# Router logits of three token tiles in one pass, gate weights held in three column strips of the array

## The chip, the cores and the metric

The kernel runs on one core of one Trainium2 chip. The metric is the device time of one launch in microseconds (us). TensorE is called PE here, its weight loads PEld; VectorE is DVE, ScalarE is ACT, GpSimd is POOL, SyncE is SP.

## The reference

A block-sparse attention feeds a mixture of experts. Cut to what matters:

```python
# attention: B, H, S, D = 4, 8, 768, 64; blocks of 32 rows; window, first, last and 3 sampled blocks are kept
scores = np.where(mask, scale * np.matmul(q, k.transpose(0, 1, 3, 2)), -1000000000.0)
attn = np.exp(scores - np.max(scores, axis=-1, keepdims=True))
attn = attn / (np.sum(attn, axis=-1, keepdims=True) + 1e-09)
x = np.matmul(attn, v)                      # reordered to N, D = 3072, 512

# experts: E, F = 8, 1024
logits = x @ w_gate
noise_scale = np.log1p(np.exp(x @ w_noise))
noisy_logits = logits + noise_scale * noise
top2 = np.argpartition(-noisy_logits, 2, axis=1)[:, :2]
...                                         # softmax weights of the two chosen experts
h = np.maximum(x[mask] @ w1[e], 0.0)
out[mask] += top2_w[mask, k, None] * (h @ w2[e])
```

The change touches only how `x @ w_gate` and `x @ w_noise` are laid on the engines.

## The kernel before, in words

**Two stages.** First comes attention, in 64 steps. A step ("macro") is four heads of one tile of 128 query rows. 24 token tiles come out of it, in four sets of T = 6 tiles. When a set is complete a routing job (`Router.run`, a generator) is advanced a few instructions at a time between the pieces of later steps (`background`); a job has one matmul group on line 635 to 639 and two on line 713. The second stage is the experts: nine blocks of rows with two matmul layers each.

**A step in program order.** `Attention.steps` writes, for step n: scores of n (PE, line 215), their row maximum (DVE, lines 250 and 269); then the transposes of step n-1's probabilities (PE, line 303, copied out by ACT, line 305); then the exponentials of n (ACT, line 291); then attention times values of n-2 (PE, line 318), then the normalisation of n-2 (DVE, lines 360 to 379). `step(n, spot)` is called with spot 0 to 3 between these pieces. Spot 1 lies behind the transposes and ahead of line 318, spot 2 behind line 318.

**A token tile behind attention.** A tile is finished every second step. Its rows are transposed by PE two steps later in four 128x128 pieces (`Router.turn`, line 548) and copied from PSUM into the tile `r_xT` (DVE, line 550). One step later `Router.logits` forms the 16 logits of each row: four accumulating matmuls with the tile as the stationary operand (128x128, fp32) and the gate weights `r_wgn` as 16 moving columns (line 560), then a small copy into `r_lc` (DVE, line 562). Both are called at spot 1. The six tiles of `r_lc` start the set's job.

**What is shared.** The PSUM tile `pe` has one buffer: transposed rows, logits and the job's matmuls use it in turn, and each waits until DVE has read the one before. While a job holds it (`router.held`), new tiles first advance the job.

**What POOL and the queues do.** For each half of a unit POOL starts an indirect load of values (`va`, line 189), behind a tiny copy `tick` (line 421) that waits for the row maximum of that step, and then copies twelve sampled key blocks next to the others (`kv`, line 205). The scores two steps later read these. Values by window (`vb`) are loaded from ACT's queue, queries from SP's.

**Experts.** From the third block on `fast1` uses seven products where there would be eight; its intermediate sums sit in tiles `um` (line 1044) and `r_xT` (line 1047), and the sums of weights in `s3` (line 862).

Of the kernel before, what the change touches and what calls it, by code (L numbers as in the profile page):

```python
# [9 lines left out]
F32 = mybir.dt.float32  # L10
# [8 lines left out]
P = 128  # L19
# [8 lines left out]
E = 8  # L28
# [5 lines left out]
OVC = OVT * P  # L34
NC = 7
NSLOT = NV * OVC
BIGIDX = 1 << 20

class Attention:
# [429 lines left out]
class Router:  # L469
# [12 lines left out]

    def consts(self, w_gate, w_noise, noise):
        nc, pool, T, B, KB = self.nc, self.pool, self.T, self.B, self.D // P
        wgn = self.wgn = pool.tile([P, KB, 2 * E], F32, name="r_wgn")
        nc.sync.dma_start(wgn[:, :, 0:E], w_gate.rearrange("(k p) e -> p k e", p=P))
        nc.sync.dma_start(wgn[:, :, E:], w_noise.rearrange("(k p) e -> p k e", p=P))
        self.noise = pool.tile([P, B, T, E], F32, name="r_noise")
        nc.sync.dma_start(self.noise.rearrange("p b t e -> p (b t e)"), noise.rearrange("p i e -> p (i e)"))

    def tables(self):
# [20 lines left out]
        self.spacer = pool.tile([1, 1], F32, name="r_spacer")  # L512
        self.tokf = pool.tile([P, B * T], F32, name="r_tokf")
        nc.vector.tensor_scalar(self.tokf, self.tok, float(-BIGIDX), None, op0=ALU.add)
        self.tab = pool.tile([P, NV * NC, 2], F32, name="r_tab")
        nc.vector.memset(self.tab, 0.0)
        self.sl = pool.tile([P, B * T, 2], I32, name="r_sl")
# [25 lines left out]
    def turn(self, i, xs, pt):  # L543

        nc = self.nc
        xv = xs.rearrange("p h d -> p (h d)")
        for kb in range(self.D // P):
            nc.tensor.transpose(pt[:, kb * P:(kb + 1) * P], xv[:, kb * P:(kb + 1) * P], self.ident)
        self.xT[i] = self.pool.tile([P, self.D // P, P], F32, name="r_xT", bufs=2)
        nc.vector.tensor_copy(self.xT[i].rearrange("p k r -> p (k r)"), pt)  # L550

    def logits(self, i, pl):

        nc, T, KB = self.nc, self.T, self.D // P
        b, t = divmod(i, T)
        if t == 0:
            self.lc[b] = self.pool.tile([P, T, 2 * E], F32, name="r_lc", bufs=2)
        xT = self.xT.pop(i)
        for kb in range(KB):
            nc.tensor.matmul(pl[:, 0:2 * E], xT[:, kb], self.wgn[:, kb], start=kb == 0, stop=kb == KB - 1,  # L560
                             skip_group_check=True)
        nc.vector.tensor_copy(self.lc[b][:, t], pl[:, 0:2 * E])

    def run(self, b, ps):

# [159 lines left out]
class Experts:  # L725
# [130 lines left out]
    def sums(self, e, s, part):  # L856
        tt = lambda o, x, y, f: self.nc.vector.tensor_tensor(o, x, y, op=f)
        a11, a12, a21, a22 = self.sums_raw(e, s)
        top, low = (self.st["wraw", e, j][0] for j in (s, s + 2))
        if part == 0:  # L860
            self.sums_split(e, s, 0, top)
            s3 = self.st["s3", e, s] = self.tsp.tile([P, 2, 256], F32, name="s3", bufs=2)
            tt(s3, a11, a21, ALU.subtract)
            tt(a21, a21, a22, ALU.add)
        elif part == 1:
            self.sums_split(e, s, 4, low)
        elif part == 2:
# [147 lines left out]
    def fast1(self, u, hook):  # L1015
        nc, H = self.nc, C // 2
# [23 lines left out]
        for p in range(self.FB // 2):  # L1040
            mul = lambda *a: self.product(u, p, *a)
            A, B, Cb = (self.ps_m.tile([P, 512], F32, name=n) for n in ("ma", "mb", "mc"))
            mul(A, 0, plain(0, 0), True)
            m = new("um", 2)
            nc.scalar.activation(m, A[:, 0:H], AF.Copy)
            mul(B, 2, mixed(1, 1), True)
            s2 = self.router.pool.tile([P, 4, P], F32, name="r_xT", bufs=2).rearrange("p k r -> p (k r)")[:, 0:H]
            add(s2, B[:, 0:H], m)
            self.flush()
            if self.rest:  # L1050
# [214 lines left out]
def kernel(ctx, tc, q, k, v, v_windows, sampled_blocks, w_gate, w_noise, noise, w1, w2, out):  # L1265
    nc = tc.nc
# [15 lines left out]
    jobs, fresh, flat = [], [], []  # L1282
    started = [0]
    now = [0]

# [7 lines left out]
    def turn_rows(n):  # L1293
        while flat and flat[0][0] <= n:
# [3 lines left out]
            router.turn(i, xs, psum[0]())  # L1298
            fresh.append((n + 1, i))

    def new_logits(n):
        while fresh and fresh[0][0] <= n:
            while router.held:
                background()
            i = fresh.pop(0)[1]
            router.logits(i, psum[0]())
            if i % T == T - 1:
                jobs.append(router.run(i // T, lambda: psum[0]()))
                started[0] += 1

    psum = [att.psum]

# [290 lines left out]
```

## Time and profile before

| | us |
|---|---|
| three timed runs, median (lowest to highest) | 866.12 (864.75 to 867.81) |
| the profiled execution, its own time | 856.92 |
| its span | 855.1 |
| PE busy | 791.1 |
| DVE busy | 549.3 |
| ACT busy | 372.6 |
| POOL busy | 360.2 |
| mean granted clock of PE, share of full speed | 0.969 |

The profiled execution took 9.2 us less than the median of the timed runs, and 1.8 us more than its own span. Attention lies between 0 and about 316 us of the span, the experts behind it. A busy share is an average over both stages.

### The profile page before, as it was taken

How to read it: one execution, taken by the hardware profiler on the slowest of the kernel's cores; microseconds unless marked ns; L12 is line 12 of the kernel's file. 1: busy time of each engine (PE TensorE's matmuls, PEld its weight loads, DVE VectorE, ACT ScalarE, POOL GpSimd, SP SyncE). 2: the span in 40 equal slices, each digit the busy share in tenths (PEclk: the TensorE clock that was granted, in tenths of full speed). 3: DMA queues.
4: the chain of work that ended last, by engine and by line, in shares of the span. 5: the costliest groups of instructions: out<-in, count | busy, mean ns of one | idle time of the engine just before them, and what ended most of it. 6: DMA issues, size and time to landing. Idle time of an engine off the chain costs nothing.

```text
span 855.1 us, 21866 instructions
## 1 busy us (share of the span) xinstructions
PE 791.1 (93%) x8889; PEld 483.4 (57%) x8889; DVE 549.3 (64%) x1122; ACT 372.6 (44%) x678; POOL 360.2 (42%) x555
## 2 busy tenths in 40 slices
PE   4899888889898878989999999999999999999996
PEld 2577676666676766548544544544544544544542
DVE  3555475756767845722558688678787786868741
ACT  2575464555565534301435445445435445435400
POOL 2534552542224520051317526537537546546431
PEclk9999898998998989999999999999999999999998
DMA  8856986695259898557845696695696695796221
GB/s 336 296 187 220 267 244 187 240 365 174 75 148 256 237 170 303 207 141 160 188 147 127 135 255 140 121 246 130 149 238 141 148 249 119 131 241 140 76 80 53
DMA packets 125021, 159.71 MB, mean 187 GB/s; under 512 B 66581, under 2 KB 83221, under 8 KB 124912
## 3 DMA queue, kind: packets, MB, share of 16 engines
q1 hardware_dynamic: 96400, 75.76, 32.6%
q0 software_dynamic: 20016, 57.47, 27.1%
q10 hardware_dynamic: 8496, 25.01, 9.3%
q8 instruction: 72, 1.18, 0.6%
q14 instruction: 37, 0.30, 0.1%
HBM read 117.30 MB, written 27.10 MB: 169 GB/s over the span
## 4 chain that ended last, share of the span: by engine, by line
PE 54%; DMA 1%; issue 1%; POOL 0%; DVE 0%; POOLq 0%
PE py L1083 26%; PE mb L1002 9%; PE ma L1002 6%; PE mc L1002 6%; PE ph L987 5%; PE py L1093 2%; DMA xtb<-xg 1%; PE py L1102 0%; DMA xg<-x_rows,gi 0%; POOL out_dram L1159 0%; DMA out_dram<-y,mt 0%; DVE y L1145 0%; PE pr L1114 0%; POOLq L1179 0%; POOLq L926 0%
## 5 line engine op out<-in xcount | busy, mean ns | idle before, releaser
L1133 POOL DMA_INDIRECT pv<-out_dram,gi x42 | 101.9, 2425 | 95.6 <-ACT pv L1127 49.3
L1002 PEld LDWEIGHTS <-wop 128*128 128x128 f16 x1008 | 98.6, 98 | 76.3
L1083 PEld LDWEIGHTS <-hh 128*128 128x128 f16 x768 | 74.5, 98 | 89.7 <-issue 2.5
L215 PE MATMUL s<-kv,q 64*32 64x192 f32 (+3 forms) x1920 | 95.9, 357 | 22.9 <-DMA kv<-in_k_dram 8.5
L305 ACT ACTIVATE t<-t 128x512 f32<-128x512 f32 (+1 forms) x120 | 63.0, 566 | 85.5 <-PE t L303 82.5
L205 POOL COPY kv<-kv 128x128 f32 x264 | 67.7, 305 | 52.9 <-issue 25.1
L1159 POOL DMA_INDIRECT out_dram<-pv,mt x42 | 51.8, 1233 | 89.2 <-DMA out_dram<-pv,mt 35.3
L1002 PE MATMUL mb<-tx,wop 128*128 128x408 f16 x432 | 83.3, 336 | 0.0
L215 PEld LDWEIGHTS s<-kv,q 64*32 64x32 f32 (+2 forms) x1920 | 52.6, 130 | 45.9 <-issue 16.6
L291 ACT ACTIVATE p<-s,nb 128x256 f32<-128x256 f32 x176 | 69.5, 477 | 19.3 <-DVE nb L269 13.8
L250 DVE TENSOR_REDUCE nm<-s 128x4 f32<-128x1024 f32 (+1 forms) x48 | 54.4, 1133 | 32.3 <-PE s L215 32.2
L1083 PE MATMUL py<-w2h,hh 128*128 128x512 f16 x192 | 72.8, 379 | 0.0
L1083 PE MATMUL py<-w1ha,hh 128*128 128x512 f16 x192 | 72.8, 379 | 0.0
L1083 PE MATMUL py<-w2l,hh 128*128 128x512 f16 x192 | 72.8, 379 | 0.0
L1083 PE MATMUL py<-w1la,hh 128*128 128x512 f16 x192 | 72.8, 379 | 0.0
L303 PE MATMUL t<-ident,p 128*128 128x128 f32 x448 | 69.1, 297 | 3.5 <-ACT t L305 3.5
L1083 PE MATMUL py<-w2h,hl 128*128 128x512 f16 x192 | 68.9, 379 | 0.0
L1083 PE MATMUL py<-w1ha,hl 128*128 128x512 f16 x192 | 68.8, 379 | 0.0
L303 PEld LDWEIGHTS t<-ident,p 128*128 128x128 f32 x448 | 51.2, 148 | 28.0 <-issue 15.7
L1007 ACT ACTIVATE hh<-us 128x408 f16<-128x408 f32 x48 | 26.1, 543 | 91.8 <-DVE us L1023 91.8
L926 POOL DMA_INDIRECT xg<-x_rows,gi x56 | 57.9, 1033 | 15.9 <-issue 15.0
L1083 PEld LDWEIGHTS <-hl 128*128 128x128 f16 x384 | 37.6, 98 | 45.3
(213 smaller groups left out, 1465.1 us busy)
## 6 DMA issues: line engine op xcount, KB each, us to landing
wraw<-in_moe_w_dram SPq DMA_DIRECT2D x64, 512.0 KB, 5.3
vb<-in_v_windows_dram ACTq DMA_DIRECT2D x28, 390.0 KB, 6.3
vb<-in_v_windows_dram ACTq DMA_DIRECT2D x14, 520.0 KB, 4.9
kv<-in_v_dram SPq DMA_DIRECT2D x4, 1560.0 KB, 17.8
q<-in_q_dram SPq DMA_DIRECT2D x12, 512.0 KB, 8.0
kv<-in_k_dram SPq DMA_DIRECT2D x8, 768.0 KB, 11.1
out_dram<-zero ACTq DMA_DIRECT2D x8, 768.0 KB, 5.1
x_rows<-x SPq DMA_DIRECT2D x20, 256.0 KB, 3.4
```

The costliest lines, as they stand in the source:

```text
L205: nc.gpsimd.tensor_copy(KG[:, j, :, 32 * s:32 * s + 32], KT[:, :, bass.ds(offs[3 * j + s], 32)])
L215: mm = lambda out, l, r, pos: nc.tensor.matmul(out, l, r, start=True, stop=True, tile_position=pos)
L250: red = lambda out, x: nc.vector.tensor_reduce(out, x, axis=AX.X, op=ALU.max, negate=True)
L291: self.nc.scalar.activation(p[:, 256 * u:256 * u + 256], S[:, a, 256 * r:256 * r + 256], AF.Exp, bias=nb[:, u:u + 1], scale=0.125)
L303: self.nc.tensor.transpose(T[i][:, c:c + P], p[:, i * w + c:i * w + c + P], self.ident)
L305: self.nc.scalar.activation(t[:, i * w:(i + 1) * w], T[i][:, 0:w], AF.Copy)
L926: g = nc.gpsimd.indirect_dma_start(out=self.xg[0:m, c], out_offset=None, in_=self.x_dram[0:nr], in_offset=bass.IndirectOffsetOnAxis(ap=r[" ...
L987: nc.tensor.matmul(ph[:, b, 0:m], w[wt][:, kb, fs], r["xt"][:, kb, a, o:o + m], start=i == 0, stop=i == last)
L1002: self.nc.tensor.matmul(bank[:, 0:H], w[:, h, o, k, cs], x(k, a), start=start and i == 0, stop=i == len(seq) - 1, skip_group_check=True)
L1083: nc.tensor.matmul(py, h[:, f, o], w[x][:, f, :], start=i == 0, stop=i == last)
L1133: g = nc.gpsimd.indirect_dma_start(out=y[0:m], out_offset=None, in_=self.out, in_offset=bass.IndirectOffsetOnAxis(ap=r["gi"][0:m, c:c + 1] ...
L1159: x = self.nc.gpsimd.indirect_dma_start(out=self.out, out_offset=bass.IndirectOffsetOnAxis(ap=self.st["u", u]["mt"][0:m, c:c + 1], axis=0) ...
```

## The change

`LG` = 3 tiles are put together in the first and second set, and of the third and fourth set the first three tiles (`grouped`): six groups, 18 tiles. For the first two tiles of a group nothing is issued at the place of the logits. At the third, `logits_of_three` holds the gate weights stationary, padded to 32 columns, in three column strips of the array, and streams each transposed tile as 128 moving columns through one strip: 12 matmuls, whose result has logits on partitions and tokens on columns. DVE copies it to `r_lt`. A step later `logits_rows` turns it back with one 128x128 transpose, and DVE picks the 48 useful columns of it. The other six tiles keep the old form. New logits are issued at spot 2 instead of spot 1, behind line 318, and the job of a full set starts when the rows are back. To make room, `r_xT` has four buffers instead of two and also takes the place of `um`, and `s3` has one buffer.

```diff
-        wgn = self.wgn = pool.tile([P, KB, 2 * E], F32, name="r_wgn")
+        wgn = self.wgn = pool.tile([P, KB, 32], F32, name="r_wgn")
+        nc.vector.memset(wgn[:, :, 2 * E:], 0.0)
...
-        self.xT[i] = self.pool.tile([P, self.D // P, P], F32, name="r_xT", bufs=2)
+        self.xT[i] = self.pool.tile([P, self.D // P, P], F32, name="r_xT", bufs=4)
...
+    def logits_of_three(self, i, pl):
+
+        nc, KB = self.nc, self.D // P
+        for kb in range(KB):
+            for c in range(LG):
+                nc.tensor.matmul(pl[32 * c:32 * c + 32, 0:P], self.wgn[:, kb], self.xT[i - LG + 1 + c][:, kb],
+                                 start=kb == 0, stop=kb == KB - 1, tile_position=(0, 32 * c), skip_group_check=True)
+        for c in range(LG):
+            del self.xT[i - c]
+        nc.vector.tensor_copy(self.lt[0:32 * LG], pl[0:32 * LG, 0:P])
+
+    def logits_rows(self, i, pl):
+
+        nc, t = self.nc, i % self.T
+        nc.tensor.transpose(pl[:, 0:P], self.lt, self.ident)
+        nc.vector.tensor_copy(self.logit_tile(i)[:, t - LG + 1:t + 1],
+                              pl[:, 0:32 * LG].rearrange("p (t e) -> p t e", e=32)[:, :, 0:2 * E])
...
-            s3 = self.st["s3", e, s] = self.tsp.tile([P, 2, 256], F32, name="s3", bufs=2)
+            s3 = self.st["s3", e, s] = self.tsp.tile([P, 2, 256], F32, name="s3", bufs=1)
...
-            m = new("um", 2)
+            m = self.router.pool.tile([P, 4, P], F32, name="r_xT", bufs=4).rearrange("p k r -> p (k r)")[:, 0:H]
...
+    def grouped(i):
+        return i // T < B - 2 or i % T < T - LG
+
     def new_logits(n):
         while fresh and fresh[0][0] <= n:
+            i = fresh.pop(0)[1]
+            if grouped(i) and i % LG < LG - 1:
+                continue
             while router.held:
                 background()
-            i = fresh.pop(0)[1]
-            router.logits(i, psum[0]())
-            if i % T == T - 1:
-                jobs.append(router.run(i // T, lambda: psum[0]()))
-                started[0] += 1
+            if grouped(i):
+                router.logits_of_three(i, psum[0]())
+                turned.append((n + 2, i))
+            else:
+                router.logits(i, psum[0]())
+                begin(i)
...
         if spot == 1:
+            logits_rows(n)
+            turn_rows(n)
+        if spot == 2:
             new_logits(n)
-            turn_rows(n)
```

How the instructions stand on PE at the third tile of the first group, before. `t` is the PSUM tile of the transposed probabilities, `po` attention times values, `s` the scores.

```order
L303 MATMUL t_1418<-ident,p 128x128 x4
L303 MATMUL t_1419<-ident,p 128x128 x4
L560 MATMUL pe<-r_wgn,r_xT 128x16 x4
L318 MATMUL po<-va_87,t 32x65 x4
...
L318 MATMUL po<-vb_89,t 32x65 x4
L215 MATMUL s<-kv_85,q 128x64 x4
```

And at the same place of the changed program (lines 304, 319 and 216 are the old 303, 318 and 215):

```order
L304 MATMUL t_1409<-ident,p 128x128 x4
L319 MATMUL po<-va_87,t 32x65 x4
...
L319 MATMUL po<-vb_89,t 32x65 x4
L576 MATMUL pe<-r_xT,r_wgn 32x128 x12
L216 MATMUL s<-kv_85,q 128x64 x4
```

The logits of one tile have gone from ahead of the eight value rows; twelve matmuls for three tiles stand behind them.

How DVE stands in that step, before and after:

```order
L250 TENSOR_REDUCE nm<-s 128x4
L269 TENSOR_SCALAR nb<-nm 128x4
L562 COPY r_lc<-pe 128x16
L360 TENSOR_SCALAR dn<-po 128x4
```

```order
L251 TENSOR_REDUCE nm<-s 128x4
L270 TENSOR_SCALAR nb<-nm 128x4
L580 COPY r_lt<-pe 96x128
L361 TENSOR_SCALAR dn<-po 128x4
```

The copy stands at the same place in DVE's queue, but now reads a result that PE makes behind the value matmuls.

The first job's group on line 635 stood a whole value piece behind the last logits before:

```order
L560 MATMUL pe<-r_wgn,r_xT 128x16 x4
L318 MATMUL po<-va_87,t 32x65 x4
...
L318 MATMUL po<-vb_89,t 32x65 x4
L635 LDWEIGHTS r_tri
L635 MATMUL pe<-r_O,r_tri 128x48
```

Now a group of three stands directly ahead of it, in the same PSUM tile (line 660 is the old 635):

```order
L576 MATMUL pe<-r_xT,r_wgn 32x128 x12
L660 LDWEIGHTS r_tri
L660 MATMUL pe<-r_O,r_tri 128x48
```

The same holds for the first job's second group of line 713 and for the second job's group of line 635.

## Rows read from the trace of the kernel before

**Rows 1.** Page, busy time by engine.

```profile
PE 791.1 (93%) x8889; PEld 483.4 (57%) x8889; DVE 549.3 (64%) x1122; ACT 372.6 (44%) x678; POOL 360.2 (42%) x555
```

**Rows 2.** Busy time by stretch: PE, PEld, DVE, ACT, POOL, PEclk, DMA, GB/s.

```profile
40.00:320.00 280.00, 245.49 (x5612) 194.25 (x5613) 177.22 (x518) 150.97 (x335) 115.94 (x331) 0.93 0.74 215
384.00:848.00 464.00, 463.42 (x2597) 239.86 (x2597) 320.17 (x448) 188.94 (x281) 217.64 (x150) 1.00 0.68 157
```

**Rows 3.** Timeline of PE, one step with logits: start, duration, instructions.

```profile
110.00 1.09 PE L303 MATMUL t<-ident,p 128*128 128x128 f32 x8
110.93 0.96 PE L560 MATMUL pe<-r_wgn,r_xT 128*128 128x16 f32 x8
111.83 0.32 PE L318 MATMUL po<-va,t 128*32 128x65 f32 x8
...
112.87 1.47 PE L215 MATMUL s<-kv,q 64*128 64x64 f32 x40
114.28 1.09 PE L303 MATMUL t<-ident,p 128*128 128x128 f32 x8
115.20 0.60 PE L548 MATMUL pe<-r_ident,xr 128*128 128x128 f32 x4
115.73 0.24 PE L318 MATMUL po<-va,t 128*32 128x65 f32 x1
```

**Rows 4.** Timeline of PE, a job's matmuls and what follows them.

```profile
159.78 1.60 PE L713 MATMUL pe<-r_val,r_hot 128*128 128x126 f32 x12
161.31 1.47 PE L215 MATMUL s<-kv,q 64*128 64x64 f32 x40
```

**Rows 5.** DVE copies from PSUM, by line: duration ns min/median/max.

```profile
L562 DVE COPY r_lc<-pe x23: 165/168/176, 43.9 to 317.3; 128x16 f32<-128x16 f32 x23
L550 DVE COPY r_xT<-pe x23: 678/684/694, 40.3 to 310.0; 128x512 f32<-128x512 f32 x23
```

**Rows 6.** Timeline of DVE and ACT in the step of rows 3.

```profile
110.27 0.69 DVE L379 TENSOR_TENSOR x<-xr,x 128x512 f16<-128x512 f32 x1 [0.70 <-ACT x L378]
110.88 1.22 DVE L250 TENSOR_REDUCE nm<-s 128x4 f32<-128x1024 f32 x1
113.12 0.84 ACT L291 ACTIVATE p<-s,nb 128x256 f32<-128x256 f32 x2
```

**Rows 7.** Timeline of POOL, and of PE's scores behind it.

```profile
79.94 0.18 POOL L421 COPY tick<-nb 1x1 f32<-1x1 f32 x1 [5.37 <-DVE r_lc L562]
83.47 2.67 POOL L205 COPY kv<-kv 128x128 f32 x11 [1.71 <-issue]
...
84.24 1.29 PE L215 MATMUL s<-kv,q 64*128 64x64 f32 x16
86.89 0.84 PE L215 MATMUL s<-kv,q 64*32 64x192 f32 x20 [0.65 <-POOL kv L205]
87.66 1.09 PE L303 MATMUL t<-ident,p 128*128 128x128 f32 x8
```

**Rows 8.** Timeline of PE, first and last waits behind logits, one between.

```profile
75.83 0.30 PE L318 MATMUL po<-vb,t 128*32 128x65 f32 x2 [1.48 <-issue]
...
171.62 0.60 PE L713 MATMUL pe<-r_val,r_hot 128*128 128x126 f32 x3 [0.87 <-DVE r_lc L562]
...
292.17 1.60 PE L713 MATMUL pe<-r_val,r_hot 128*128 128x126 f32 x12 [1.44 <-DVE r_lc L562]
```

**Rows 9.** Stretches around two stalls, columns as in rows 2.

```profile
84.30:87.60 3.30, 2.45 (x41) 1.29 (x40) 1.54 (x4) 1.48 (x4) 3.15 (x11) 1.00 0.71 183
94.40:98.70 4.30, 2.35 (x48) 1.15 (x40) 1.46 (x4) 1.50 (x4) 1.54 (x7) 1.00 0.86 230
99.50:106.00 6.50, 6.50 (x116) 5.46 (x114) 1.72 (x6) 2.66 (x6) 3.11 (x11) 0.50 1.01 343
106.20:110.00 3.80, 3.80 (x116) 3.15 (x116) 2.75 (x6) 3.05 (x7) 2.08 (x7) 1.00 0.37 97
```

**Rows 10.** Timeline in the experts: DVE writes `s3` (s), ACT reads it, DVE's next.

```profile
507.51 0.68 DVE L857 TENSOR_TENSOR s<-wraw 128x512 f32<-128x512 f32 x1
...
509.92 0.61 ACT L837 ACTIVATE wop<-s 128x512 f16<-128x512 f32 x1
...
520.74 0.68 DVE L857 TENSOR_TENSOR s<-wraw 128x512 f32<-128x512 f32 x1
```

More of the change, by code (lines that the diff above doesn't have):

```diff
@@ L36 @@
 NSLOT = NV * OVC
+LG = 3
 BIGIDX = 1 << 20
@@ L484, in consts @@
         nc, pool, T, B, KB = self.nc, self.pool, self.T, self.B, self.D // P
-        wgn = self.wgn = pool.tile([P, KB, 2 * E], F32, name="r_wgn")
+        wgn = self.wgn = pool.tile([P, KB, 32], F32, name="r_wgn")
+        nc.vector.memset(wgn[:, :, 2 * E:], 0.0)
         nc.sync.dma_start(wgn[:, :, 0:E], w_gate.rearrange("(k p) e -> p k e", p=P))
-        nc.sync.dma_start(wgn[:, :, E:], w_noise.rearrange("(k p) e -> p k e", p=P))
+        nc.sync.dma_start(wgn[:, :, E:2 * E], w_noise.rearrange("(k p) e -> p k e", p=P))
         self.noise = pool.tile([P, B, T, E], F32, name="r_noise")
@@ L514, in tables @@
         nc.vector.tensor_scalar(self.tokf, self.tok, float(-BIGIDX), None, op0=ALU.add)
+        self.lt = pool.tile([P, P], F32, name="r_lt")
+        nc.vector.memset(self.lt, 0.0)
         self.tab = pool.tile([P, NV * NC, 2], F32, name="r_tab")
@@ L548, in turn, with logit_tile @@
             nc.tensor.transpose(pt[:, kb * P:(kb + 1) * P], xv[:, kb * P:(kb + 1) * P], self.ident)
-        self.xT[i] = self.pool.tile([P, self.D // P, P], F32, name="r_xT", bufs=2)
+        self.xT[i] = self.pool.tile([P, self.D // P, P], F32, name="r_xT", bufs=4)
         nc.vector.tensor_copy(self.xT[i].rearrange("p k r -> p (k r)"), pt)
+    def logit_tile(self, i):
+        b = i // self.T
+        if b not in self.lc:
+            self.lc[b] = self.pool.tile([P, self.T, 2 * E], F32, name="r_lc", bufs=2)
+        return self.lc[b]
     def logits(self, i, pl):
[L554 to L557, printed above, removed]
+        nc, KB = self.nc, self.D // P
         xT = self.xT.pop(i)
         for kb in range(KB):
-            nc.tensor.matmul(pl[:, 0:2 * E], xT[:, kb], self.wgn[:, kb], start=kb == 0, stop=kb == KB - 1,
+            nc.tensor.matmul(pl[:, 0:2 * E], xT[:, kb], self.wgn[:, kb, 0:2 * E], start=kb == 0, stop=kb == KB - 1,
                              skip_group_check=True)
-        nc.vector.tensor_copy(self.lc[b][:, t], pl[:, 0:2 * E])
+        nc.vector.tensor_copy(self.logit_tile(i)[:, i % self.T], pl[:, 0:2 * E])
+    def logits_of_three(self, i, pl):
+        nc, KB = self.nc, self.D // P
+        for kb in range(KB):
[10 more added lines that the diff above has]
+                              pl[:, 0:32 * LG].rearrange("p (t e) -> p t e", e=32)[:, :, 0:2 * E])
     def run(self, b, ps):
@@ L1043, in fast1 @@
             mul(A, 0, plain(0, 0), True)
-            m = new("um", 2)
+            m = self.router.pool.tile([P, 4, P], F32, name="r_xT", bufs=4).rearrange("p k r -> p (k r)")[:, 0:H]
             nc.scalar.activation(m, A[:, 0:H], AF.Copy)
             mul(B, 2, mixed(1, 1), True)
-            s2 = self.router.pool.tile([P, 4, P], F32, name="r_xT", bufs=2).rearrange("p k r -> p (k r)")[:, 0:H]
+            s2 = self.router.pool.tile([P, 4, P], F32, name="r_xT", bufs=4).rearrange("p k r -> p (k r)")[:, 0:H]
             add(s2, B[:, 0:H], m)
@@ L1281 @@
     zero = rp.tile([P, DM], F32, name="zero")
-    jobs, fresh, flat = [], [], []
+    jobs, fresh, flat, turned = [], [], [], []
     started = [0]
@@ L1299, in turn_rows, with begin, logits_rows @@
             fresh.append((n + 1, i))
+    def grouped(i):
+        return i // T < B - 2 or i % T < T - LG
+    def begin(i):
+        if i % T == T - 1:
+            jobs.append(router.run(i // T, lambda: psum[0]()))
+            started[0] += 1
     def new_logits(n):
         while fresh and fresh[0][0] <= n:
+            i = fresh.pop(0)[1]
+            if grouped(i) and i % LG < LG - 1:
+                continue
             while router.held:
                 background()
-            i = fresh.pop(0)[1]
-            router.logits(i, psum[0]())
-            if i % T == T - 1:
-                jobs.append(router.run(i // T, lambda: psum[0]()))
-                started[0] += 1
+            if grouped(i):
[4 more added lines that the diff above has]
+                begin(i)
+    def logits_rows(n):
+        while turned and turned[0][0] <= n:
+            while router.held:
+                background()
+            i = turned.pop(0)[1]
+            router.logits_rows(i, psum[0]())
+            begin(i)
     psum = [att.psum]
```

## The prediction

> **What bounds the kernel now.** I read the page first: PE is busy for 791.1 us of the 855.1 us span, so work taken from PE looks like time [rows 1]. Then I cut the span into its stages. Behind 384 us, in the experts, PE is busy for 463.4 of 464 us at the full granted clock [rows 2]; nothing of the change's PE work lies there, so this stage only has to be kept from harm. In attention, from 40 to 320 us, PE is busy for 245.5 of 280 us, at a mean granted clock of 0.93 [rows 2]. The clock has two levels, 1.0 and 0.5, so 0.07 / 0.5 = 14% of that stage ran at the half level. PE is the busiest engine there, but three loops run beside it, and what the change is worth depends on how far behind PE they are.
>
> The next view is the timeline of one step [rows 3]. Transposes begin at 110.00, logits at 110.93, value matmuls at 111.83, the next scores at 112.87 and the next transposes at 114.28. PE does not pause, and the logits hold it for 0.90 us. The following step has row transposes in that place, 0.53 us (115.20 to 115.73). A pair of steps is thus bound by PE at some 8 us, as long as all else keeps up.
>
> **The two loops that hardly keep up.** The first runs over DVE and ACT. In the step with logits DVE still has to finish the rows of the last tile (line 379, 110.27), starts the row maximum only at 110.88, and ACT ends the exponentials at 113.12 + 0.84 = 113.96 [rows 6]. The transposes that need them start at 114.28 [rows 3]. So this loop has 0.32 us to spare, in the very step that loses 0.90 us. The scores from which it starts lie ahead of the logits, so taking these out does not start it earlier.
>
> The second loop runs over POOL. At 79.94 the tick sees the row maximum; the key copies run to 83.47 + 2.67 = 86.14, and a little on in a twelfth copy. The scores that need them began at 84.24 and are only done when the transposes start at 87.66, 3.42 us where an unhindered one takes 1.41 (112.87 to 114.28) [rows 3, 7]. Here PE waits for 2 us already, and 0.90 us less work ahead of it makes a longer wait.
>
> **What is taken off PE.** 18 tiles lose the old form: 18 x 0.90 = 16.2 us [rows 3].
>
> **What is added on PE, first bound.** A group has 12 matmuls of 128 fp32 columns. The nearest row for one of them alone is the job's: six matmuls of 126 columns in 161.31 - 159.78 = 1.53 us, 0.255 us each, so 0.26 us for 128 [rows 4]. If the three strips run side by side, a group takes four rounds, 4 x 0.26 = 1.04 us; if they run one behind the other, 12 x 0.26 = 3.1 us. The nearest row for strips is the value piece: 32 matmuls of 65 columns, in four strips of 32 columns, take 112.87 - 111.83 = 1.04 us, 0.033 us each [rows 3], where one alone would take 0.255 x 65 / 126 = 0.13 us. That is fully side by side, four for one, and the new matmuls have the same strips and the same depth. I take 1.04 us and keep 3.1 for the range. The transpose back is one of the four of rows 3: 0.53 / 4 = 0.13 us. Together 6 x 1.17 = 7.0 us, so PE has 9.2 us less work.
>
> The Trainium skill ("TensorE: Matmul & The Clock Gate", Part 3, Measured speedup vs the span model) gives 2.38 times for three column strips of 512 columns, not 3. By it a group would take an estimated 12 x 0.26 / 2.38 = 1.31 us and the sum below would lose 6 x 0.27 = 1.6 us; the trace's four for one differs from it, and I go by the trace.
>
> **DVE, POOL, queues.** DVE loses 18 copies of 0.168 us, 3.0 us. It gets six copies of 128 columns and six of 48; between 0.168 us for 16 columns and 0.684 us for 512 these lie at 0.28 and 0.20 us, together 2.9 us [rows 5]. Even. The two memsets stand in the first steps, where PE has yet to wait for its loads; their bounds are nothing and one copy of 0.28 us each, and I take nothing. Each group makes DVE wait at its `r_lt` copy until PE is through, about 1.04 us behind the value piece, and the normalisation queues behind it. It holds back rows of the first half of a tile, which are not cast yet, and 1.41 us of scores run meanwhile, so this is hidden. No DMA is added, and no queue is passed in another order.
>
> **The PSUM tile `pe`.** Three job groups now stand directly behind a group of three. PE must wait there for the end of the matmuls and for the DVE copy, 0.28 us plus hand-overs: between 0.3 and the 1.44 us of the longest such wait [rows 8]. I take 0.5, near the bound, because DVE's queue is empty there: 1.5 us. Such waits go elsewhere: 0.87 us at 171.62 and 1.44 us at 292.17 were waits for the copy of old logits [rows 8]. Between them and the new ones I book nothing.
>
> **Experts.** `s3` is written at 507.51, read by ACT at 509.92 and written again at 520.74 [rows 10]: a second buffer covers 10 us that are not needed. `um` and `r_xT` had two buffers each and now share four in strict turn, so each still has two. Both cost nothing; without this slack one copy of some 0.7 us (rows 10) would show twelve times, 8 us.
>
> **The sum.** PE's places that are emptied are 12: the first two tiles of each group. Where PE runs at half clock all else has time: from 99.5 to 106.0 it is busy for all 6.5 us [rows 9]. There a place is worth twice 0.90, 1.8 us, and all of it is gained. With 14% of the stage at this level (rows 2), 12 x 0.14 = 1.7; I count two places, 3.6 us. The other ten lie between 0 (POOL or a value load ends last), 0.32 (DVE and ACT end last) and 0.90 (nothing does). Five of the emptied places are followed within a step or two by a PE wait, the first at 75.83 and the last at 292.17 [rows 8], so they give nothing. Of the other five I give 0.32 to four and 0.90 to one: 2.2 us. Against this the six third places are longer by 1.04 - 0.90 = 0.14 us and the six row transposes cost 0.13 us, which add 1.6 us. The sum is 3.6 + 2.2 - 1.6 = 4.2 us less: the profiled execution's 856.9 us becomes 852.7. The timed runs lie 9.2 us above that execution, without the trace showing why; I carry the difference over unchanged, 866.1 - 4.2 = 861.9 us.
>
> **Rivals.**
> (A) The forecast, 861.9 us, 859 to 863.5 by itself: half-clock places counted from one to three. Chance 0.42.
> (B) Swallowed. All twelve places end before POOL's key copies or a value load. For it: the 2 us wait of rows 7. Against it: DVE and PE alone fill steps like that of rows 3. Only the half-clock gain, less what is added, is left: 3.6 - 1.6 = 2.0 us, or none, so 864 to 866. Chance 0.30.
> (C) All of it passes, 9.2 us, as if nothing but PE counted: 857 us. For it: PE's 88% in the stage. Against it: the 0.32 us of rows 6. Chance 0.10.
> (D) The other side: the clock. Before the fall at 99.5 PE was busy for only 2.35 of 4.3 us; at 84.3 to 87.6, 2.45 of 3.3 us, it did not fall [rows 9]. Freed time that only lengthens a wait makes stalls of the second kind into the first. One more stretch of 6.5 us at half the clock costs 3.25 us. With the gain swallowed, two such stretches give 866.1 + 6.5 - 1 = 871.6 us; it decides from the first new one on. Chance 0.13. The Trainium skill ("TensorE: Matmul & The Clock Gate", HAM oscillation) states this as a rule, idle gaps between bursts of matmuls throw the clock back; the trace agrees, with 0.50 behind the stall.
> (E) The strips run one behind the other: 6 x (3.1 + 0.13) = 19.4 us for the 16.2 taken out, 3.2 us slower, 869.3 us. Against it: the value piece. Chance 0.05.
>
> **How the numbers follow.** A change within 0.3%, 2.6 us, can hardly be told from none with this measurement. Faster than 863.5 are A and C, 0.52; same is B, 0.30; slower are D and E, 0.18. The range of 857 to 869 holds A and B, half of C, and of D and E the part with one stretch or a partly hidden cost; some 2 in 10 are left outside.
>
> **What would show it.** In the changed kernel's trace: a group of three in about 1.04 us from its start to the next scores, not 3.1; the transpose back at 0.13; in emptied steps the transposes on PE starting right behind ACT's exponentials, or longer waits of scores for `kv`; waits of some 0.5 us ahead of three job groups; experts as long as before, with PE at 99% and more; and a half-clock share of attention near 14%. I would be wrong if that share moves by more than a few per cent, since one stretch weighs nearly as much as the whole gain, or if the job's later start, one to two steps, lets its DVE work fall on steps that have less room.

## The result and the profile after

The changed kernel is slower: 872.38 us median (11 runs, 866.48 to 880.13) against 864.75 us (11 runs, 861.20 to 870.42), ratio 1.0087 with a 95% interval of 1.0059 to 1.0115. That is some 7.5 us more, where 4.2 us less were forecast, and it lies outside the range of 857 to 869.

The page's busy times of the changed kernel answer to [rows 1].

```profile
PE 791.7 (91%) x8895; PEld 476.1 (54%) x8895; DVE 549.4 (63%) x1118; ACT 372.5 (43%) x678; POOL 354.3 (41%) x555
```

The same two stretches as in [rows 2], columns as there.

```profile
40.00:320.00 280.00, 234.85 (x5406) 178.87 (x5408) 173.58 (x497) 148.12 (x330) 117.10 (x331) 0.93 0.71 211
384.00:848.00 464.00, 455.76 (x2552) 236.27 (x2551) 318.48 (x446) 188.88 (x281) 215.49 (x154) 1.00 0.68 160
```

PE is busy 10.6 us less in the stretch of attention, in part only because the changed kernel's attention ends behind it (the first expert matmul comes at 328.0 us and not at 316.7). From 40 us up to that matmul PE is busy for 242.0 of 288.0 us in the changed kernel and for 242.6 of 276.7 before: what grew is the time in which it waits. The mean granted clock of the stretch is 0.93 in both kernels. PE's timeline shows the new instructions: a group and the scores behind it, a row transpose and the values behind it, and the first matmul of a job behind a group.

```profile
77.38 1.05 PE L576 MATMUL pe<-r_xT,r_wgn 128*32 128x128 f32 x24
78.36 1.56 PE L216 MATMUL s<-kv,q 64*128 64x64 f32 x40
...
85.36 0.27 PE L585 MATMUL pe<-r_ident,r_lt 128*128 128x128 f32 x1
85.56 0.32 PE L319 MATMUL po<-va,t 128*32 128x65 f32 x8
...
209.63 0.18 PE L660 MATMUL pe<-r_O,r_tri 128*128 128x48 f16 x1 [0.40 <-DVE r_lt L580]
```

From start to the next start a group holds PE for 0.98 us and a row transpose for 0.20 us, and the job waits 0.40 us. The row transpose stands two steps behind its group (`n + 2` in the diff; "a step later" above is one too few), so the first two jobs start two steps later than before. What was added is as small as forecast. What was not forecast is in PE's list of waits between 40 and 320 us (what waits, on which line, for whom: us in total, times, longest). Four rows of before:

```profile
PE t L303 <- ACT t L305: 2.2, 5, 0.8
PE pe L548 <- DVE r_tab L716: 2.0, 2, 1.0
PE pe L548 <- DVE r_A L642: 1.7, 2, 1.0
...
PE pe L713 <- DVE r_val L707: 0.7, 1, 0.7
```

The same view of the changed kernel:

```profile
PE po L319 <- DVE xr L367: 5.2, 4, 2.4
PE t L304 <- ACT t L306: 3.1, 4, 2.2
PE pe L552 <- DVE r_tab L741: 3.0, 3, 1.3
...
PE pe L738 <- DVE r_val L732: 2.4, 2, 1.3
PE pe L552 <- DVE r_A L667: 2.3, 2, 1.3
...
PE s L216 <- ACT p L283: 1.3, 1, 1.3
PE pe L660 <- DVE r_lt L580: 0.8, 2, 0.4
```

Value matmuls that wait for the normalisation (`xr`) are not in before's list, here they take 5.2 us: 1.9 us at 196.59 and 201.81, where DVE has work of the second set's job ahead of the normalisation, and 3.3 us at 271.12 and 286.17, where it has work of the third set's. The waits for the job's own DVE results grew from 4.4 to 7.7 us. To find where the time goes, one event that every kernel has as often can be followed, the 56 starts of the row maximum `nb` (counted from 0), and the first expert matmul (`first ph`). From the traces, us:

```
                nb 30   nb 35   nb 41   nb 42   nb 54   first ph
before          171.3   200.0   234.0   237.6   301.4   316.7
changed         164.1   194.5   232.8   240.6   307.2   328.0
changed-before   -7.2    -5.5    -1.2    +3.0    +5.8   +11.3
```

The changed kernel is 7 us ahead at nb 30, and it has lost this and 3 us more by nb 42. One single step, from 41 to 42, takes 7.8 us in it and 3.6 before; the rest is spread. (Between the last two columns 5.5 us more come from something else, told at the end. The pair of traces differs by 18.5 us, the timed medians by 7.6; the profiled execution of before was shorter than every timed run of it.)

**That step, read engine by engine.** DVE's timeline in the changed kernel:

```profile
226.64 0.17 DVE L270 TENSOR_SCALAR nb<-nm 128x2 f32<-128x2 f32 x1
226.72 0.28 DVE L741 TENSOR_TENSOR r_tab<-r_tab,pe 128x126 f32<-128x126 f32 x1
226.91 0.55 DVE L723 TENSOR_TENSOR r_eq<-r_io,r_cf 128x378 f32<-128x378 f32 x1
227.37 1.04 DVE L726 TENSOR_TENSOR r_hot<-r_io,r_pm 128x768 f32<-128x768 f32 x1
228.34 0.64 DVE L730 TENSOR_TENSOR r_val<-r_eq,r_tokf 128x378 f32<-128x378 f32 x1
228.90 0.63 DVE L732 TENSOR_TENSOR r_val<-r_eq,r_pay 128x378 f32<-128x378 f32 x1
229.45 0.15 DVE L361 TENSOR_SCALAR dn<-po 128x4 f32<-128x4 f32 x1
...
229.85 0.89 DVE L367 TENSOR_TENSOR xr<-po,rc 128x128 f32<-128x128 f32 x3
```

Four instructions of the second set's routing job (`r_eq` to the second `r_val`, 2.54 us from 226.91 to 229.45) stand ahead of the denominators `dn` and the normalisation `xr`, though PE had left the value matmuls for the next scores at 228.01. ACT's timeline, first the changed kernel, then before:

```profile
230.78 0.63 ACT L379 ACTIVATE x<-xr 128x512 f16<-128x512 f32 x1 [1.88 <-DVE xr L367]
...
232.72 1.07 ACT L306 ACTIVATE t<-t 128x384 f32<-128x384 f32 x2 [0.55 <-PE t L304]
```

```profile
232.02 0.63 ACT L378 ACTIVATE x<-xr 128x512 f16<-128x512 f32 x1 [0.19 <-DVE xr L366]
```

ACT waits 1.88 us for `xr`, where it waited 0.19, and its copies of the transposed probabilities `t` are queued behind. PE's timeline, changed and before:

```profile
228.77 0.88 PE L304 MATMUL t<-ident,p 128*128 128x128 f32 x6
231.84 1.42 PE L304 MATMUL t<-ident,p 128*128 128x128 f32 x6 [2.19 <-ACT t L306]
233.05 2.63 PE L738 MATMUL pe<-r_val,r_hot 128*128 128x126 f32 x12
235.62 0.88 PE L216 MATMUL s<-kv,q 64*64 64x384 f32 x8
237.77 0.66 PE L552 MATMUL pe<-r_ident,xr 128*128 128x128 f32 x4 [1.27 <-DVE r_tab L741]
```

```profile
231.70 0.87 PE L303 MATMUL t<-ident,p 128*128 128x128 f32 x6
233.08 0.93 PE L303 MATMUL t<-ident,p 128*128 128x128 f32 x6 [0.51 <-ACT t L305]
233.94 0.88 PE L215 MATMUL s<-kv,q 64*64 64x384 f32 x8
```

PE's next six transposes wait 2.19 us for ACT, not 0.51; the job's matmuls, 1.5 us long in [rows 4], now take 2.57; and the row transposes wait 1.27 us for `r_tab`, whose addition DVE does only behind a row maximum. The granted clock goes with the long matmuls (stretches of the changed kernel, columns as in rows 2):

```profile
228.80:231.80 3.00, 0.84 (x12) 0.60 (x6) 2.21 (x8) 1.12 (x4) 2.85 (x8) 1.00 0.06 7
232.00:235.40 3.40, 3.40 (x18) 3.40 (x17) 0.90 (x3) 1.87 (x5) 0.00 (x0) 0.50 0.93 269
```

Behind 3 us in which PE was busy for 0.84 it runs 3.4 us at half clock.

In before the same four instructions of DVE and the job's matmuls run in an earlier step, because the job starts two steps earlier. The first of the four and the matmuls, and the `nb` 40 of before:

```profile
223.06 0.55 DVE L698 TENSOR_TENSOR r_eq<-r_io,r_cf 128x378 f32<-128x378 f32 x1
225.45 1.60 PE L713 MATMUL pe<-r_val,r_hot 128*128 128x126 f32 x12 [0.67 <-DVE r_val L707]
229.57 0.17 DVE L269 TENSOR_SCALAR nb<-nm 128x2 f32<-128x2 f32 x1 [0.46 <-ACT t L305]
```

The wait for ACT lies ahead of `nb` 41, so the sum is taken from `nb` 40 (226.64 in the changed kernel) to `nb` 42: 13.9 us, and 8.0 before, 5.9 us more. The wait for ACT is 1.7 us longer, the transposes behind it take 1.21 us from start to next start for 0.86, the job's matmuls stand here with 2.57 us, and `r_tab` is waited for 1.27 us: 1.7 + 0.35 + 2.57 + 1.27 = 5.9. Some 1.5 us of this is only moved, the matmuls' own length at the full clock; the waits and the half clock are the loss.

### The profile page after: what moved, and what is told of

Its sections match the earlier page's. It is cut to its first block, busy times and chain, and to the rows that moved or that the text cites. A ratio compares the mean times of both kernels' runs of the same rounds, so it can differ in the third digit from the quotient of the medians.

```text
span 873.6 us, 21873 instructions
## 1 busy us (share of the span) xinstructions
PE 791.7 (91%) x8895; PEld 476.1 (54%) x8895; DVE 549.4 (63%) x1118; ACT 372.5 (43%) x678; POOL 354.3 (41%) x555
## 4 chain that ended last, share of the span: by engine, by line
PE 73%; DVE 9%; issue 5%; another core or an unknown queue 3%; DMA 3%; ACT 2%; POOL 2%; POOLq 1%; SPq 1%; ACTq 0%; DVEq 0%
PE py L1108 26%; PE mb L1027 9%; PE ph L1012 7%; PE ma L1027 6%; PE s L216 6%; PE mc L1027 6%; PE po L319 4%; PE t L304 4%; PE py L1118 2%; DVE nm L251 2%; DMA kv<-in_k_dram 2%; DMA wraw<-in_moe_w_dram 1%; PE pe L738 1%; POOL kv L206 1%
## 5 line engine op out<-in xcount | busy, mean ns | idle before, releaser
L1158 POOL DMA_INDIRECT pv<-out_dram,gi x42 | 89.4, 2129 | 98.6 <-ACT pv L1152 57.2
L1184 POOL DMA_INDIRECT out_dram<-pv,mt x42 | 55.3, 1316 | 93.2 <-DMA out_dram<-pv,mt 37.5
L304 PE MATMUL t<-ident,p 128*128 128x128 f32 x448 | 72.0, 306 | 4.5 <-ACT t L306 4.4
L304 PEld LDWEIGHTS t<-ident,p 128*128 128x128 f32 x448 | 53.6, 153 | 29.9 <-issue 17.6
L319 PE MATMUL po<-va,t 128*32 128x65 f32 x1408 | 51.3, 228 | 16.5 <-issue 10.6
L1184 POOL DMA_INDIRECT out_dram<-y,mt x14 | 13.9, 991 | 123.7 <-DVE y L1150 84.6
```

The source lines that it names most:

```text
L304: self.nc.tensor.transpose(T[i][:, c:c + P], p[:, i * w + c:i * w + c + P], self.ident)
L319: mm = lambda o, n, hl, l, r, start, stop: self.nc.tensor.matmul(O[o:o + n, hl], l, r, start=start, stop=stop, tile_position=(0, o))
L1158: g = nc.gpsimd.indirect_dma_start(out=y[0:m], out_offset=None, in_=self.out, in_offset=bass.IndirectOffsetOnAxis(ap=r["gi"][0:m, c:c + 1] ...
L1184: x = self.nc.gpsimd.indirect_dma_start(out=self.out, out_offset=bass.IndirectOffsetOnAxis(ap=self.st["u", u]["mt"][0:m, c:c + 1], axis=0) ...
```

## The experiments

Each batch of runs had one chip, and its ratios are to the kernel before on that chip, whose medians were 857.40 us (e1 to e4), 863.34 (e5 to e8), 859.04 (e9 to e12) and 857.39 (e13 to e15). Diffs are against the kernel named.

**e1, memory only.** Before, with the new tiles and buffers (`r_wgn` 32 wide, `r_lt`, four buffers of `r_xT`, one of `s3`, `um` drawn from `r_xT`) and the old computation:

```diff
-        self.xT[i] = self.pool.tile([P, self.D // P, P], F32, name="r_xT", bufs=2)
+        self.xT[i] = self.pool.tile([P, self.D // P, P], F32, name="r_xT", bufs=4)
...
-            m = new("um", 2)
+            m = self.router.pool.tile([P, 4, P], F32, name="r_xT", bufs=4).rearrange("p k r -> p (k r)")[:, 0:H]
```

> The kernel before with only the changes of memory: gate weights padded to 32 columns and their memset, the unused tile r_lt, r_xT with four buffers that also take um, s3 with one. Theory of the later jobs: none of the loss is here, ratio to before 0.998 to 1.002. Rival, the experts' shared buffers cost: the two PE waits of 1.4 and 1.7 us on DVE behind line 1048 are here too, and the ratio is 1.003 to 1.004.

858.10 us, ratio 1.0008 (0.9976 to 1.0040). Memory shows no cost. The rival's 1.003 to 1.004 lies at the interval's end, but the two waits that it named are not in this run's trace, where PE waits for nothing in the experts.

**e2, all singles.** Changed kernel without any group; single logits stand behind the values, and both jobs start at their old step:

```diff
-        return i // T < B - 2 or i % T < T - LG
+        return False
```

> The changed kernel with no tile grouped: all 24 tiles one by one, but their logits behind the value matmuls instead of ahead of them, each set's job at its old step. Theory of the later jobs: 0.998 to 1.003, since the jobs start in the old steps. Rival, the new place of the logits costs, since DVE's normalisation queues behind a copy that waits for PE: most of the loss is here, 1.005 to 1.009.

853.82 us, ratio 0.9987 (0.9950 to 1.0025). No loss without groups and without the later start.

**e3, jobs later.** The reverse: before, single logits at their old place, and the jobs of the first two sets start two steps later:

```diff
-                jobs.append(router.run(i // T, lambda: psum[0]()))
-                started[0] += 1
+                ripe.append((n + 2 if i // T < B - 2 else n, i))
+                begin(n)
```

`begin(n)`, also called at spot 1 of every step, starts a job of `ripe` once its step has come.

> The kernel before, all logits in the old form and place, but the jobs of the first and second set start two steps later, as in the changed kernel. Theory of the later jobs: the second set's job falls on the dense steps of the second head pair and costs 6 to 10 us, ratio 1.007 to 1.012. Rival, the loss comes from less PE work and a clock that falls, or from the group of three itself: 0.998 to 1.002, because PE's work is that of before.

866.51 us, ratio 1.0103 (1.0073 to 1.0134). The whole loss, with not one group in the kernel.

**e4, second set's last three single.** Changed kernel; the second set's job is back at its old step, five groups stay:

```diff
-        return i // T < B - 2 or i % T < T - LG
+        return i // T < 1 or i % T < T - LG
```

> The changed kernel with the last three tiles of the second set one by one as well, so that this set's job starts at its old step; five groups are left. Theory of the later jobs: the loss of the second head pair's dense steps goes, 0.992 to 0.998, faster than before. Rival, PE's freed time brings the clock down: as slow as the changed kernel, 1.005 to 1.010, since five of six groups are still there.

860.52 us, ratio 1.0038 (1.0013 to 1.0064). By the middle values more than half of the loss is gone, but the run missed its forecast of faster than before: with the first set's job still late and five groups, it stays slower.

**e5, four groups.** Changed kernel; both jobs are at their old steps, four groups stay (`return i % T < T - LG`).

> The changed kernel, but in every set only the first three tiles make a group and the last three go one by one, so four groups are left and both jobs start at the step at which they started before. Theory (the jobs of the first two sets pay for their later start, the groups themselves cost nothing): no slower than before, ratio 0.993 to 0.999. Rival (the groups cost what the result shows, by their place in the step, by the clock or by the waits that they make): about two thirds of the loss stays, ratio 1.005 to 1.007.

864.12 us, ratio 1.0020 (0.9986 to 1.0055). The rival's 1.005 lies at the interval's upper end, and the gain that the theory allowed did not come: four sixths of the prediction's 4.2 us would be 0.9968, below the interval.

**e6, rows in the same step.** All six groups; the group is back ahead of the values and the row transpose behind them in the same step:

```diff
-                turned.append((n + 2, i))
+                turned.append((n, i))
...
         if spot == 1:
-            logits_rows(n)
+            new_logits(n)
             turn_rows(n)
         if spot == 2:
-            new_logits(n)
+            logits_rows(n)
```

> The changed kernel with all six groups, but a group and its row transpose stand in one step: the group back at the old place ahead of the value matmuls, the row transpose behind them, so that both jobs start in the step of before (at its end, not ahead of the value matmuls). Theory (later start): ratio 0.992 to 1.000. Rival (groups cost by themselves): 1.005 or more, since PE now waits in the same step for the copy of the group's logits.

862.66 us, ratio 0.9989 (0.9955 to 1.0023). Six groups show no cost when the jobs start on time, and no gain clear of noise either.

**e7 and e8, one job later.** As e3, for the second set alone (`i // T == 1`) and the first set alone (`i // T == 0`).

> The kernel before, in which the job of the second set alone starts two steps later; nothing else is changed. Theory that the second set's job does most of it, because two steps later its pieces fall on the crowded steps at the row maxima 37 to 42: ratio 1.005 to 1.008. If both jobs share the loss of about 1%: 1.004 to 1.006. If the first set's job alone did it: within 0.3% of 1.

> The kernel before, in which the job of the first set alone starts two steps later. Theory that the second set's job does most of it: ratio 1.000 to 1.003. If both share: 1.004 to 1.006. If the first set's job alone did it: 1.008 to 1.011. If the two together make up for less or more than the 1.0103 of both later, they are not additive.

e7: 869.07 us, ratio 1.0068 (1.0033 to 1.0104). e8: 864.73 us, ratio 1.0018 (0.9985 to 1.0052). The second set's job does most of it; 0.68 + 0.18 = 0.86% is near e3's 1.03%.

**e9, second table half moved.** Changed kernel; six empty slices ahead of the four instructions shown above, so that on DVE `r_eq` stands behind the normalisation and the others behind the next row maximum:

```diff
+            for _ in range(6 if b == 1 and t else 0):
+                yield
             eq = tile([P, G, 2, K], F32, "eq")
```

> The changed kernel; in the second set's job alone six empty slices stand ahead of the second table half, so that on DVE its r_eq, r_hot and two r_val no longer stand in front of a tile's denominators and normalisation but behind them. Theory (the place of these 2.5 us on DVE makes the value transposes wait 2.19 us for ACT, and the clock falls there): that wait goes, and the ratio to before falls from 1.0087 to 1.002 to 1.005, since the waits at 200 to 213 us stay. Rival (the loss is spread over all late slices): 1.007 or more. Against both, r_val now stands ahead of the next row maximum of the dense rows and could delay that one instead.

860.27 us, ratio 1.0017 (0.9984 to 1.0049). The time fell as the theory had it, a little further even, but PE's timeline did not follow it:

```profile
228.88 0.93 PE L304 MATMUL t<-ident,p 128*128 128x128 f32 x6 [0.77 <-ACT t L306]
...
233.74 2.92 PE L740 MATMUL pe<-r_val,r_hot 128*128 128x126 f32 x12 [2.54 <-DVE r_xT L554]
```

The wait for ACT fell to 0.77 us, and a new one of 2.54 us stands ahead of the job's matmuls. In this execution nb 41 to 42 takes 8.6 us, no less than in the changed kernel. So the run is no proof of the place, and e13 to e15 were made for it.

**e10, a quarter of the logits.** Before; in the 18 tiles only one of four blocks of the contraction is formed, which takes 54 x 0.225 = 12.2 us of work from PE and adds nothing anywhere:

```diff
+        KB = 1 if b < self.B - 2 or t < T - 3 else KB
         for kb in range(KB):
```

> The kernel before with one of four blocks of the contraction in the logits of the 18 tiles, so that their places on PE are 0.23 us long instead of 0.90, 12 us of PE work less in attention, and nothing stands elsewhere: the other three blocks are left out, so the logits are those of a quarter of the row. It prices freed PE time alone. If PE set the pace of all these places: 12 us less, ratio 0.986. By the steps of the prediction (two places at the half clock, ten between 0 and 0.3 or 0.9): about 5 us less, 0.994. Rival B, freed time is swallowed by the other loops: 0.998 to 1.000.

856.05 us, ratio 0.9969 (0.9944 to 0.9994), 2.7 us (0.5 to 4.8). Of PE time freed here about a fifth reaches the end, half of the 5 us that the prediction's steps gave. The logits differ, so rows go to other experts; PE's instructions fall only by the 108 of these 54 matmuls, two records each (x8781 for x8889).

**e11, the job far later.** As e7 with seven steps in place of two.

> The kernel before, in which the second set's job starts seven steps later, so that its second table half falls behind the dense rows. Theory (not the lateness costs but the step on which the table work falls): less than at two steps later, 0.999 to 1.004. Rival (lateness itself costs, through the queue of jobs or the gathers that wait for them): 1.007 or more.

862.14 us, ratio 1.0026 (1.0002 to 1.0050), less than at two steps by the middle values; but the two intervals overlap, and this run too is slower than before. That lateness by itself costs nothing is not shown.

**e12, rows one step earlier.** Changed kernel with all six groups:

```diff
-                turned.append((n + 2, i))
+                turned.append((n + 1, i))
```

> The changed kernel with the row transpose one step earlier, in the step behind its group instead of two behind, so that the second set's table work stands on DVE where it stood before. Theory: the loss is gone, ratio 0.993 to 1.001. Rival (the groups cost by themselves): 1.005 or more.

855.44 us, ratio 0.9958 (0.9927 to 0.9989): faster than before, by 3.6 us. PE's transposes at the place of the step above, and one of PE's waits between 40 and 320 us that the changed kernel's list has not:

```profile
225.08 0.93 PE L304 MATMUL t<-ident,p 128*128 128x128 f32 x6 [0.31 <-ACT t L306]
```

```profile
PE pe L552 <- DVE r_lc L586: 7.0, 6, 2.1
```

The wait for ACT is 0.31 us, and nb 41 to 42 takes 3.7 us, as before. What it pays instead are 7.0 us of row transposes that wait for the copy of the logits just ahead of them, since both now use `pe` in one spot. The jobs still start one step later than before.

**e13, e14, e15, the place.** All three on the kernel before. e13 holds back only the second set's table part, by 16 empty slices (two steps), the front of the job stays. e14 leaves both jobs alone and adds four DVE operations of the tables' shapes, whose results nobody reads, ahead of the normalisation behind the second table half. e15 adds the same four at `n == 51`, where DVE waits for scores.

```diff
+        for _ in range(16 if b == 1 else 0):
+            yield
         K, G = NV * NC, T // 2
```

```diff
+        if n == 47 and spot == 2:
+            router.again()
         FENCE[:] = [2, 2] if n < NS - 11 else [1, 1]
```

> The kernel before, in which the second set's job starts at its old step and only its table part is held back by 16 empty slices, two steps, so that the second half's r_eq, r_hot and two r_val stand on DVE where they stand in the changed kernel, ahead of a tile's normalisation. Theory (the place of the table work is the cost): nearly all of what the whole job cost when it came two steps later, ratio 1.004 to 1.007. Rival (the front of the job costs, its waits at 200 to 213 us): within 0.2% of 1.

> The kernel before with both jobs as they are; four DVE operations of the table's shapes (2.5 us), whose results nobody reads, are added at that same place, ahead of the normalisation behind the second table half. Theory: PE's value transposes wait some 2 us longer for ACT, and more if the clock falls there: 2 to 5 us, ratio 1.002 to 1.006. Rival (that place has room): within 0.1% of 1.

> The same four operations four steps later, where DVE waited 1.95 us for scores. Theory: at most 0.6 us, ratio 0.999 to 1.001. If DVE work costs wherever it stands: as much as at the first place.

e13: 860.50 us, ratio 1.0045 (1.0014 to 1.0077). e14: 860.27 us, ratio 1.0015 (0.9980 to 1.0050). e15: 857.12 us, ratio 0.9986 (0.9955 to 1.0018). PE's timeline at the place, e13 and then e14:

```profile
228.86 0.93 PE L303 MATMUL t<-ident,p 128*128 128x128 f32 x6 [2.21 <-ACT t L305]
229.62 1.50 PE L715 MATMUL pe<-r_val,r_hot 128*128 128x126 f32 x12
231.05 0.88 PE L215 MATMUL s<-kv,q 64*64 64x384 f32 x8
233.20 0.66 PE L548 MATMUL pe<-r_ident,xr 128*128 128x128 f32 x4 [1.27 <-DVE r_tab L718]
```

```profile
231.56 0.93 PE L303 MATMUL t<-ident,p 128*128 128x128 f32 x6 [1.93 <-ACT t L305]
```

e13 brings back both waits of the changed kernel, 2.21 and 1.27 us, and two thirds of what e7 lost, without a late front. In e14 the wait for ACT alone appears, 1.93 us in place of 0.51, by nothing but DVE work in that place; the 1.4 us by which it is longer are 0.17% of the time, and the ratio says 0.15%, less than the 0.2 to 0.6% expected, and its interval takes in no change as well. By time alone e14 and e15 can't be told apart. What the place does to PE's wait is shown, what it costs in the end is shown by e13 alone.

Every trace shows the stretch from `nb` 40 to `nb` 42. Before and the nine runs with the second set's job on time or one step late and nothing added here take 7.8 to 8.4 us; e14 takes 9.5, e11 11.7, e3 and e13 12.3, and e7, e9 and the changed kernel 13.8 to 13.9. The loss of the step thus comes and goes with the late job, groups or none. But e9 and e11 lose 5.8 and 3.7 us here and are slower by only 1.5 and 2.2 us, so this step alone does not set the time.

## Why the prediction was wrong

**The step that failed** is the costing of DVE, POOL and queues, "together 2.9 us. Even". It counted how much DVE work the change adds and takes, and left out which work it moves. The two jobs that start two steps later carry their DVE instructions and matmuls with them; the sum has no term for that. The last paragraph named it ("lets its DVE work fall on steps that have less room"), with no price and no chance, and neither the DVE order in the second set's job nor the room in the steps on which it would fall was looked up. By e3 the term is +1.03% or 9 us (6.3 to 11.5), which is more than the whole sum; e7 and e8 give 5.9 us of it to the second set's job, e13 3.9 us (1.2 to 6.6) to that job's table part. e6 takes the later start away, e12 one of its two steps by a single number, both keep all groups, and the loss is gone. That much is shown. With e12's gain the sums fit: 3.6 us less and 8.8 more (e3) are 5.2 more, and 5.1 to 9.9 were measured. How the late job's work turns into time is shown in part: the table part's place (e13) gives some two thirds of e7's loss, with wide intervals on both.

**The emptied places** held in kind, and their size stays open. That most of the freed time is swallowed is shown by e10, and rival C, all of it passing, is out by it; but its 2.7 us for 12.2 us of freed PE work are half of what the prediction's steps give for it. The sum gave 4.2 us less; with the jobs one step late (e12) it is 3.6 us less (0.9 to 6.3), while e5 and e6, with the jobs on time, show no gain clear of noise. e12 moves singles behind the values too, which alone (e2) gave no measurable gain. Rival B, some 2.0 us less or none, fits these runs as well as the forecast does. That ACT and POOL do the swallowing, as the prediction argued, is not shown: PE's waits for `kv` between 40 and 320 us are 4.8 us before, 2.8 in the changed kernel and 5.6 in e12.

**The group** was right: 0.98 us for 1.04, side by side, and rival E (3.1 us) is out. Twelve matmuls at the job's 0.26 us would be 3.1 us, so the group is 3.2 times as fast as that row. Three strips side by side can give 3 at most, so the job's row, whose stationary operand is 128 columns wide and not 32, is not quite the right unit. The 2.38 times of the Trainium skill ("TensorE: Matmul & The Clock Gate", Part 3, Measured speedup vs the span model), by which a group would take an estimated 1.31 us, differs from the trace, and the measured 0.98 decides. The row transpose took 0.20 us for 0.13, 0.4 us over six.

**The waits of the jobs for `pe`** behind a group were 0.39 to 0.40 us for 0.5, right. Booking nothing between old and new waits for logits was safe: the jobs' matmuls waited 2.9 us for `r_lc` before and wait 1.2 us for `r_lt` now. What was not booked are the waits for `r_tab`, `r_val` and `r_A`, which grew by 3.3 us.

**The wait at the copy of the group's logits** was about right: in four of six groups the copy starts 1.10 to 1.26 us behind the group's first matmul, in the others 1.8 and 2.0, for 1.04. DVE is idle for 14.3 us ahead of the six copies, but half of this is one wait, in the stall told at the end:

```profile
314.40 0.29 DVE L580 COPY r_lt<-pe 96x128 f32<-96x128 f32 x1 [7.01 <-PE pe L576]
```

e6 and e12 have such waits too and lose nothing.

**Clock.** Rival D had freed PE time as the cause of new stretches at half clock. The stretch at 232.0 lies behind a stall that the late job made. e13 has the same instructions there in the same order, and its matmuls behind the stall take 2.19 us (transposes and job, 228.86 to 231.05) where the changed kernel takes 3.78 (231.84 to 235.62): 1.6 us for the half clock. The stall and what follows it in e13, then what follows it in e7 (columns as in rows 2):

```profile
225.80:228.80 3.00, 0.85 (x14) 0.61 (x6) 2.21 (x8) 1.11 (x4) 2.85 (x8) 1.00 0.12 11
228.86:232.30 3.44, 3.07 (x26) 2.21 (x26) 1.37 (x4) 1.93 (x5) 0.03 (x1) 1.00 0.94 259
```

```profile
237.60:241.00 3.40, 3.40 (x19) 3.09 (x21) 0.47 (x2) 1.71 (x4) 0.00 (x0) 0.50 1.01 321
```

So the half clock follows this stall in the changed kernel and e7, not in e13 (nor in e3), and is no fixed part of the loss. The rule of the Trainium skill ("TensorE: Matmul & The Clock Gate", HAM oscillation), idle gaps between bursts of matmuls throw the clock back, agrees with the first two (in the changed kernel 0.84 of 3.00 us busy, then 0.50) and not with e13 (0.85 of 3.00, then 1.00).

That D is out altogether is not shown. The clock of attention is 0.93 in both profiles, but in the timed runs the mean of a whole launch is lower with the jobs late (e3 0.964, before on that chip 0.972; e7 0.970 and 0.973), and also in e4 and e5, which keep groups and have the second set's job on time (0.965 and 0.966 for 0.972 and 0.973), while e12 is level (0.971). Some of e3's loss, and the gain that e4 and e5 lack, may lie there; before's clock in the runs beside the changed kernel's is not known.

**Experts.** Nothing was booked for memory, and e1 bears it out. The prediction's sign of experts "as long as before" failed all the same: the changed kernel's trace has 8.0 us of waits there (for `xtb`, `hl` and `us`) that before's has not. Waits for `xtb`, the second block's rows, of 2.1 to 5.1 us also stand in e3, e7, e9, e11 and e13, all with the second set's job late, and in e5 and e8, and in none of the other profiles. e3, e7, e8, e11 and e13 have before's memory. Whether they are part of what the late job costs stays open: no run tests it, and the block starts some 12 us behind the last addition to `r_tab` with such a wait (12.0 in the changed kernel, 12.4 in e13) as without (11.9 before, 12.2 in e12).

**Still open.** How the remaining third of e7's loss splits over the front of the job: in the changed kernel the waits of 1.33, 1.29 and 1.33 us at 201.81, 204.22 and 212.10 lie there, and e7 has three like them (1.2, 1.3 and 1.3), but no run held back the front alone. e9's fall by 0.7% is not explained by its trace. And what the waits for `xtb` and the lower clock add to the late job's cost is not separated.

## What to carry to other kernels

An edit that makes a result ready later moves all that starts from it: print the order of the engines' instructions before and after, and look which instruction on the path now has foreign work ahead of it. Equal sums of busy time say nothing about that; one job's table part two steps late (e13, 3.9 us) takes as much as all six groups give (e12, 3.6 us). When a change with a sound saving comes out slower, try first to start the displaced work earlier: one number (the row transpose one step sooner) turned 1.0087 into 0.9958, each against before on its own chip.

## What the runs showed that was not expected

One stall of a kind of its own: value matmuls wait in small pieces for nothing that the trace shows. The waits of that form between 295 and 320 us, changed kernel and e7:

```profile
PE po L319 <- issue: 3.9, 6, 1.1
```

```profile
PE po L318 <- issue: 3.1, 7, 0.5
```

In the changed kernel the eight value rows from 305.80 (32 matmuls, two records each) take 6.6 us, where they take 1.04 in [rows 3]. The profiles of the changed kernel and of e5 to e8 have such a series there; those of before, e1 to e4 and e9 to e15 have none. From `nb` 54 to the first expert matmul the five take 18.2 to 20.8 us, the others 11.5 to 16.4. It seems to go with the chip and not with the kernel: e5 to e8 ran where before's median was 863.34 us, and the changed kernel's runs stand beside 864.75 us of before, the other experiments beside 857 to 859 us. That would explain some 5 of the 9.2 us between before's profiled execution and its timed runs, but before was not profiled on the chip of e5 to e8, so it stays open. It also means that the pair of traces (18.5 us) shows more than the change does (7.6 us).
